# Attention logits split by heads over two steps, phi and the second weighing moved behind dense matmuls, in a kernel of linear-memory attention beside a token-mixing MLP

## The chip, the cores and the metric

The kernel runs on one core of one Trainium2 chip. The metric is the device time of one execution in microseconds (us). The core's engines are called as the profile calls them: PE is the matmul engine (PEld its weight loads), ACT the scalar engine, DVE the vector engine, POOL the one that makes the masks here, SP the one that issues most DMAs.

A ratio is the mean time of one kernel's runs over the mean of the other's of the same rounds, so it is not quite the ratio of the medians that are quoted beside it.

## The reference, cut to what matters

```python
def _A_ref(x, wq, wk, wv, wo, beta):           # x: 1 x 2048 x 1024, already normalised
    H, Dh, N, L = 32, 32, 4, 512               # 4 segments of 512 tokens
    q, k, v = ...                              # x @ wq, wk, wv, by heads and segments
    phi = lambda t: jnp.where(t > 0, t + 1.0, jnp.exp(t))
    M, z = 0, 0
    for s in range(N):
        logits = einsum('bhqd,bhkd->bhqk', qs, ks) * scale + mask     # causal inside the segment
        a_dot = softmax(logits) @ vs
        a_mem = (phi(qs) @ M) / (phi(qs) @ z + 1e-06)
        o = g * a_mem + (1.0 - g) * a_dot
        M = M + phi(ks)^T @ vs;  z = z + sum(phi(ks))
    return o @ wo
def _B_ref(x, w1, b1, w2, b2): ...             # LayerNorm, then gelu(w1) and w2 over the token axis
return x + _A_ref(xn, ...) + _B_ref(xn, ...)   # ... marks cuts
```

## The kernel before

After a head (LayerNorm and the first MLP product, up to 217 us) the kernel runs 32 *units*: one segment and a group of four heads each. A unit makes logits in two *steps*, exponentiates them on ACT, masks them on POOL, and weighs v in four *weighings* (one for each block of 128 queries), which DVE evicts. Two units ahead, q and k are projected, and v where needed. The gaps are filled with *dense* matmuls of 128x128 by 512 columns, from the second MLP product and from the product with wo (`main_emit(n)` emits n of them; `share(u)` says how many at each of three places). A tail ends the program.

Logits have a contraction of only 32, so four heads use four row groups of PE at once (`tile_position`). The kernel never lets two row groups write one PSUM bank at the same time (the prediction names the page that asks for this). Key block 2 (256 columns for each head) has two heads in a bank, hence the explicit wait:

```python
    LOGIT_STEPS = [[[(0, 2), (2, 2)], [(1, 0), (3, 0), (0, 0), (2, 0)], [(1, 2), (3, 2)]],
                   [[(0, 1), (1, 1), (2, 1), (3, 1), (0, 3), (1, 3), (2, 3), (3, 3)]]]

    def logits(self, u, step):

        fw = self.fw
        k = u % 3
        toks = []
        for group in self.LOGIT_STEPS[step]:
            if len(toks) == 2:
                fw.E["pe"].eng.wait_ge(toks[0].sem, toks[0].val)
            banks = self.R_bank[4:6] if group[0][1] == 2 else self.R_bank[0:4]
            with fw.group(reads=[self.R_kT[k], self.R_qT[k]], writes=banks) as grp:
                for r, kb in group:
                    n_q = SEG_L - P * kb
                    b, col = (4 + r // 2, 256 * (r % 2)) if kb == 2 else (r, 384 if kb == 3 else 0)
                    fw.mm(self.ps[:, b, col:col + n_q], self.kT[k][32 * r:32 * r + 32, kb * P:(kb + 1) * P],
                          self.qT[k][32 * r:32 * r + 32, kb * P:SEG_L],
                          start=True, stop=True, tile_position=(32 * r, 0))
            toks.append(grp.tok)
        heads = self.ps[:, 0:4, :]
        if step == 0:
            self.weights((0,), heads, self.R_bank[0:4])
            self.weights((2,), self.ps[:, 4:6, :].rearrange("p b (h q) -> p (b h) q", q=256), self.R_bank[4:6])
        else:
            self.weights((1, 3), heads, self.R_bank[0:4])

    def weights(self, kbs, src, R_src):
        fw = self.fw
        off, total = PT_OFF[kbs[0]], sum(SEG_L - P * kb for kb in kbs)
        fw.op("act", lambda e: e.activation(self.pT[:, :, off:off + total], src, ACT.Exp, scale=SCALE),
              reads=R_src, writes=[self.R_pTu[kb] for kb in kbs] + [self.R_pTd[kb] for kb in kbs])
        for kb in kbs:
            d = self.pT[:, :, PT_OFF[kb]:PT_OFF[kb] + P]
            fw.op("pool", lambda e: e.affine_select(d, d, pattern=[[0, 4], [1, P]], compare_op=ALU.is_ge,
                                                    fill=0.0, base=0, channel_multiplier=-1),
                  reads=[self.R_pTu[kb]], writes=[self.R_pTd[kb]])
```

Projections; phi follows directly (`phi` is two DVE operations on `etmp`):

```python
    def proj_q(self, u, b):
        fw = self.fw
        w, R_w = self.wq_ring.get(u)
        self.proj(w, R_w, u, b)
        k = u % 3
        fw.op("act", lambda e: e.activation(self.qT[k][:], self.bank(b), ACT.Copy),
              reads=[self.R_bank[b]], writes=[self.R_qT[k]])
        if u >= N_GRP:
            fw.op("act", lambda e: e.activation(self.etmp[0][:], self.bank(b), ACT.Exp),
                  reads=[self.R_bank[b]], writes=[self.R_etmp[0]])
            self.phi(self.pqT[k][:], self.R_pqT[k], self.qT[k][:], self.R_qT[k], 0)

    def proj_k(self, u, b):
        fw = self.fw
        w, R_w = self.wk_ring.get(u)
        self.proj(w, R_w, u, b)
        k = u % 3
        fw.op("dve", lambda e: e.tensor_copy(self.kT[k][:], self.bank(b)),
              reads=[self.R_bank[b]], writes=[self.R_kT[k]])
        if u // N_GRP < N_SEG - 1:
            fw.op("act", lambda e: e.activation(self.etmp[1][:], self.bank(b), ACT.Exp),
                  reads=[self.R_bank[b]], writes=[self.R_etmp[1]])
            self.phi(self.mtmp[1][:], self.R_mtmp[1], self.kT[k][:], self.R_kT[k], 1)
```

The loop over units and the shares (the parts around it are cut):

```python
        for u in range(N_UNIT):
            s = u // N_GRP
            un, m = u + self.LEAD, u // 4 + 1
            n0, n1, n2 = self.share(u)
            if u == N_GRP:
                wait = _after(*[self.R_xnT[c] for c in range(4)])
                self.oT[1] = self.xnT[0]
                self.R_oT[1] = [Res(f"oT1_{g}", wait) for g in range(N_GRP)]
            self.logits(u, 0)
            if u and last_of_seg(u - 1):
                self.o_transpose_dma(u - 1)
            self.main_emit(n0)
            if u and not last_of_seg(u - 1):
                self.combine(u - 1)
            self.logits(u, 1)
            if u + 1 < N_UNIT and (u + 1) // N_GRP < N_SEG - 1:
                self.k_transpose(u + 1)
            if u and not last_of_seg(u - 1):
                self.o_transpose_dma(u - 1)
            self.main_emit(n1)
            self.weigh(u, 0)
            self.weigh(u, 1)
            if un < N_UNIT:
                self.proj_q(un, 0)
            else:
                self.main_emit(8)
            self.weigh(u, 2)
            if m < 2 * N_SEG:
                self.proj_v(m, u % 4, 2)
            self.weigh(u, 3)
            if un < N_UNIT:
                self.proj_k(un, 1)
            if last_of_seg(u):
                self.combine(u)
            self.main_emit(n2)
    ...
    def share(u):
        if u < N_UNIT - 4:
            return (11, 14, 7) if u < N_GRP else (11, 15, 8)
        return (11, 16, 10) if u < N_UNIT - 2 else (11, 16, 4) if u < N_UNIT - 1 else (11, 13, 7)
```

The softmax here doesn't subtract the row's maximum and nothing guards it: scores larger than these inputs give would overflow.

## Time and profile before

| | before |
|---|---|
| time, three runs | 699.18, 700.11, 700.43 us (median 700.11) |
| span of the profiled run | 698.3 us |
| first real matmul | 7.20 us |
| first logits, unit 0 | 217.55 us |
| one middle unit (484.06 to 499.14) | 15.09 us |
| PE gap before the last transposes | 0.47 us |

From the page of the kernel before, part 1 (busy time and share by engine) and the shares of part 4 (the chain of waits that ended last):

```profile
PE 687.9 (99%) x4740; PEld 327.3 (47%) x4830; DVE 260.3 (37%) x581; ACT 273.9 (39%) x301; POOL 104.8 (15%) x156
...
PE 96%; DMA 1%; issue 1%; DVE 1%; SPq 1%
```

A busy PE isn't yet a full PE, because the ends of matmuls are modelled. Starts are measured. In the trace, dense matmuls that follow each other start 0.2158 us apart. "TensorE: Matmul & The Clock Gate" of the Trainium skill (Part 1) gives 215.7 ns for 512 columns at the warm clock, and this trace agrees. A middle unit has 58 of them (12.52 us), 40 weighing matmuls of 25 ns (1.01 us), eight small memory matmuls (0.45 us) and the logits (1.08 us), together 15.06 of the measured 15.09 us.

Two stretches of the timeline of PE before, with start, duration and count, show both logit steps of a unit:

```profile
483.74 0.38 PE L194 MATMUL ps_all<-gT,w2h_898 128*128 128x512 bf16 x1
484.06 0.63 PE L194 MATMUL ps_all<-qT_1551,kT_1554 32*128 32x256 bf16 x8
484.62 1.90 PE L194 MATMUL ps_all<-gT,w2h_898 128*128 128x512 bf16 x8
486.35 0.81 PE L194 MATMUL ps_all<-gT,w2h_897 128*128 128x512 bf16 x3
487.10 0.40 PE L194 MATMUL ps_all<-qT_1551,kT_1554 32*128 32x384 bf16 x8
487.43 0.82 PE L194 MATMUL ps_all<-gT,w2h_897 128*128 128x512 bf16 x3
```

Read each step from the end of the dense matmul ahead (its start plus 0.2158) to the start of the next dense one. Step 0: 483.74 + 0.22 = 483.96 to 484.62, 0.66 us. Step 1: 486.35 + 3 x 0.2158 = 487.00 to 487.43, 0.43 us. The first 0.10 us of each pass before the first logit matmul starts.

ACT before, groups by shape between 250 and 690 us (count, busy us, mean ns, then idle time before them):

```profile
L810 ACT ACTIVATE pT<-ps_all 128x2048 bf16<-128x2048 f32 x59 | 110.7, 1877 | 56.1 <-PE ps_all L194 55.1
L810 ACT ACTIVATE pT<-ps_all 128x1024 bf16<-128x1024 f32 x29 | 29.5, 1018 | 0.0
L746 ACT ACTIVATE etmp_1567<-ps_all 128x512 bf16<-128x512 f32 x24 | 14.2, 592 | 0.0
```

The tail before, PE and then DVE. PE is idle for 0.47 us because the transposes wait for `o_s`. On DVE a bias add (`stg`) and then the last evictions run ahead of the chain that makes it:

```profile
681.28 0.22 PE L194 MATMUL ps_all<-MZbf,pqT_1558 128*128 128x132 bf16 x1
681.33 2.97 PE L194 MATMUL ps_all<-wo_sb,xnT_70 128*128 128x512 bf16 x13
684.77 0.40 PE L200 MATMUL ps_all<-ident,o_s_1566 128*128 128x128 bf16 x4 [0.47 <-DVE o_s_1566 L890]
```

```profile
680.71 0.75 DVE L954 SCALAR_TENSOR_TENSOR stg_1573<-ps_all,b2c,stg_1573 128x512 bf16<-128x512 f32 x1 [1.00 <-PE ps_all L194]
681.38 0.76 DVE L848 CAST ost_1564<-ps_all 128x264 bf16<-128x264 f32 x2
...
684.28 0.43 DVE L890 TENSOR_TENSOR o_s_1566<-prod 128x512 bf16<-128x512 bf16 x1
```

The head before, weight loads of PE. Each load stands for one matmul, so loads 0.43 us apart mean half the clock. The ten warming matmuls (`warm`, zeros) are over at 5.5 us, and the first real ones, from 7.17, are slow as well, until about 9.9 us:

```profile
4.64 0.15 PEld L194 LDWEIGHTS ps_all<-warm 128*128 128x128 bf16 x1 [0.28 <-issue]
7.17 0.14 PEld L194 LDWEIGHTS ps_all<-h,w1early 128*128 128x128 bf16 x2 [2.37 <-DMA w1early<-in_B_w_dram]
7.58 0.15 PEld L194 LDWEIGHTS ps_all<-h,w1early 128*128 128x128 bf16 x1 [0.27 <-issue]
...
10.04 2.04 PEld L194 LDWEIGHTS ps_all<-h,w1early 128*128 128x128 bf16 x10 [0.19 <-issue]
```

### The profile page before, as it was taken

How to read it: one execution, taken by the hardware profiler on the slowest of the kernel's cores; microseconds unless marked ns; L12 is line 12 of the kernel's file. 1: busy time of each engine (PE TensorE's matmuls, PEld its weight loads, DVE VectorE, ACT ScalarE, POOL GpSimd, SP SyncE). 2: the span in 40 equal slices, each digit the busy share in tenths (PEclk: the TensorE clock that was granted, in tenths of full speed). 3: DMA queues.
4: the chain of work that ended last, by engine and by line, in shares of the span. 5: the costliest groups of instructions: out<-in, count | busy, mean ns of one | idle time of the engine just before them, and what ended most of it. 6: DMA issues, size and time to landing. Idle time of an engine off the chain costs nothing.

```text
span 698.3 us, 11182 instructions
## 1 busy us (share of the span) xinstructions
PE 687.9 (99%) x4740; PEld 327.3 (47%) x4830; DVE 260.3 (37%) x581; ACT 273.9 (39%) x301; POOL 104.8 (15%) x156
## 2 busy tenths in 40 slices
PE   8999999999999999999999999999999999999998
PEld 3444444444444444444444445444445444444444
DVE  6740000000012334333455545546545553444545
ACT  7531111112234445444455344455444345434440
POOL 2500000000001112211122211112211112211130
PEclk9999999999999999999999999999999999999999
DMA  8487774327036438457263634526273533445004
GB/s 307 116 194 182 167 211 119 93 60 140 1 119 134 102 72 137 102 101 139 46 137 79 129 87 93 128 52 131 63 150 79 97 95 73 113 77 121 19 21 136
DMA packets 210553, 77.17 MB, mean 111 GB/s; under 512 B 173128, under 2 KB 202824, under 8 KB 210504
## 3 DMA queue, kind: packets, MB, share of 16 engines
q1 hardware_dynamic: 210280, 76.29, 48.3%
q8 instruction: 38, 0.62, 0.4%
q10 hardware_dynamic: 224, 0.16, 0.1%
q14 instruction: 11, 0.09, 0.1%
HBM read 59.79 MB, written 5.24 MB: 93 GB/s over the span
## 4 chain that ended last, share of the span: by engine, by line
PE 96%; DMA 1%; issue 1%; DVE 1%; SPq 1%
PE ps_all L194 96%; DMA xin<-in_A_x_dram 1%; SPq L216 1%; DVE prod L886 0%; DVE stg_1573 L954 0%; DVE ost_1564 L848 0%; DVE h L661 0%; DVE o_s_1566 L890 0%; PE ps_all L200 0%; DVE srec L884 0%; DVE fin_7812 L1047 0%; DVE srec L883 0%; DVE srec L885 0%; DVE ln_mv L644 0%; DVE ln_st L622 0%
## 5 line engine op out<-in xcount | busy, mean ns | idle before, releaser
L810 ACT ACTIVATE pT<-ps_all 128x2048 bf16<-128x2048 f32 (+1 forms) x96 | 149.4, 1591 | 58.3 <-PE ps_all L194 57.2
L814 POOL TENSOR_SCALAR_AFFINE_SELECT pT<-pT 128x512 bf16<-128x512 bf16 x128 | 88.3, 703 | 554.8 <-ACT pT L810 553.7
L717 ACT ACTIVATE gT<-ps_all,b1c 128x512 bf16<-128x512 f32 x56 | 37.7, 689 | 139.3 <-PE ps_all L194 133.8
L755 DVE CAST kT_1554<-ps_all 128x512 bf16<-128x512 f32 x11 | 7.6, 690 | 170.6 <-PE ps_all L194 170.6
L194 PE MATMUL ps_all<-h,w1s_80 128*128 128x512 bf16 x251 | 55.6, 379 | 0.3
L194 PE MATMUL ps_all<-h,w1s_81 128*128 128x512 bf16 x251 | 55.6, 379 | 0.3
L194 PE MATMUL ps_all<-h,w1s_79 128*128 128x512 bf16 x250 | 55.4, 379 | 0.3
L194 PE MATMUL ps_all<-gT,w2h_897 128*128 128x512 bf16 x219 | 54.3, 380 | 0.4
L194 PE MATMUL ps_all<-gT,w2h_895 128*128 128x512 bf16 x221 | 53.7, 380 | 0.2
L194 PE MATMUL ps_all<-gT,w2h_896 128*128 128x512 bf16 x214 | 53.0, 380 | 0.6 <-issue 0.2
L194 PE MATMUL ps_all<-gT,w2h_898 128*128 128x512 bf16 x215 | 52.7, 379 | 0.5 <-issue 0.2
L848 DVE CAST ost_1563<-ps_all 128x264 bf16<-128x264 f32 (+1 forms) x64 | 23.8, 394 | 56.2 <-PE ps_all L194 56.0
L194 PEld LDWEIGHTS ps_all<-h,w1s_80 128*128 128x128 bf16 x256 | 25.0, 98 | 30.2
L194 PEld LDWEIGHTS ps_all<-h,w1s_79 128*128 128x128 bf16 x256 | 25.0, 98 | 30.2
L194 PEld LDWEIGHTS ps_all<-h,w1s_81 128*128 128x128 bf16 x256 | 25.0, 98 | 30.2
L848 DVE CAST ost_1564<-ps_all 128x264 bf16<-128x264 f32 (+1 forms) x64 | 23.7, 393 | 39.1 <-PE ps_all L194 38.9
L758 ACT ACTIVATE etmp_1568<-ps_all 128x512 bf16<-128x512 f32 x24 | 14.3, 597 | 58.8 <-DVE kT_1556 L755 20.7
L194 PEld LDWEIGHTS ps_all<-gT,w2h_898 128*128 128x128 bf16 x224 | 21.1, 98 | 25.5 <-issue 1.3
L194 PEld LDWEIGHTS ps_all<-gT,w2h_896 128*128 128x128 bf16 x224 | 20.9, 98 | 25.8 <-issue 1.7
L194 PEld LDWEIGHTS ps_all<-gT,w2h_895 128*128 128x128 bf16 x224 | 20.8, 98 | 25.2 <-issue 1.3
L194 PEld LDWEIGHTS ps_all<-gT,w2h_897 128*128 128x128 bf16 x224 | 20.7, 98 | 24.9 <-issue 1.3
L194 PE MATMUL ps_all<-wo_sb,oT_1571 128*128 128x512 bf16 x125 | 31.1, 379 | 0.2
(154 smaller groups left out, 843.7 us busy)
## 6 DMA issues: line engine op xcount, KB each, us to landing
w1s_81<-in_B_w_dram SPq DMA_DIRECT2D x4, 1024.0 KB, 5.8
w1s_79<-in_B_w_dram SPq DMA_DIRECT2D x4, 1024.0 KB, 5.6
w1s_80<-in_B_w_dram SPq DMA_DIRECT2D x4, 1024.0 KB, 5.7
wq_891<-in_A_wq_dram SPq DMA_DIRECT2D x16, 256.0 KB, 5.5
wq_892<-in_A_wq_dram SPq DMA_DIRECT2D x16, 256.0 KB, 3.5
wk_893<-in_A_wk_dram SPq DMA_DIRECT2D x16, 256.0 KB, 5.3
wk_894<-in_A_wk_dram SPq DMA_DIRECT2D x16, 256.0 KB, 3.8
w2h_895<-in_B_w_dram SPq DMA_DIRECT2D x8, 448.0 KB, 4.8
```

Source lines behind the costliest of these rows:

```text
L194: ins = self.nc.tensor.matmul(*args, **kwargs)
L216: ins = es.eng.dma_start(out_ap, in_ap, transpose=True) if transpose else es.eng.dma_start(out_ap, in_ap)
L717: fw.op("act", lambda e: e.activation(self.gT[:, fc, half * 512:(half + 1) * 512], self.bank(b), ACT.Gelu_apprx_tanh, bias=self.b1c[:, fc: ...
L755: fw.op("dve", lambda e: e.tensor_copy(self.kT[k][:], self.bank(b)), reads=[self.R_bank[b]], writes=[self.R_kT[k]])
L758: fw.op("act", lambda e: e.activation(self.etmp[1][:], self.bank(b), ACT.Exp), reads=[self.R_bank[b]], writes=[self.R_etmp[1]])
L810: fw.op("act", lambda e: e.activation(self.pT[:, :, off:off + total], src, ACT.Exp, scale=SCALE), reads=R_src, writes=[self.R_pTu[kb] for ...
L814: fw.op("pool", lambda e: e.affine_select(d, d, pattern=[[0, 4], [1, P]], compare_op=ALU.is_ge, fill=0.0, base=0, channel_multiplier=-1), ...
L848: fw.op("dve", lambda e: e.tensor_copy(dst, self.ps[:, b, 0:n * VW]), reads=[self.R_bank[b]], writes=[self.R_ost[o][qb]])
```

## The change

The intent is to take the semaphore wait out of the logits. Key block 2 is split by heads: heads 0 and 2 in step 0, heads 1 and 3 in step 1, so that within a step no bank has two row groups. Its exp is split with it, and step 1 now waits for both exps of step 0, so more dense matmuls stand between the steps. The exps for phi read q and k from SBUF, so their PSUM banks come free earlier. Phi itself and the second weighing move behind dense work. Besides, the shares now add up exactly to the 1088 dense matmuls that there are, and the first chunk of x comes by one DMA instead of two halves issued by SP and ACT. The diff, cut to its core (the bookkeeping of resources is left out):

```diff
@@
         for fp in range(N_FCH // 2):
             self.w1_ring.srcs.append(self.B_w1[:, fp * 256:(fp + 1) * 256].rearrange("(c p) f -> p c f", p=P))
         self.R_w1e = [Res(f"w1e{c}") for c in range(N_TCH)]
-        for h, issuer in enumerate(("sp", "act")):
-            fw.dma(self.xin[64 * h:64 * h + 64, 0, :], self.x_d[64 * h:64 * h + 64, 0, :],
-                   writes=[(self.R_xin[0], self.R_xin0)[h]], issuer=issuer)
         fw.op("act", lambda e: e.activation(self.junk[:, 0:1], self.warm[:, 0:1], ACT.Gelu_apprx_tanh),
               reads=[self.R_warm], writes=[self.R_junk])
-        for kind, c0, n in (("x", 1, 1), ("x", 2, 1), ("w", 0, 2), ("x", 3, 1), ("x", 4, 2), ("w", 2, 2), ("x", 6, 2),
+        for kind, c0, n in (("x", 0, 1), ("x", 1, 1), ("x", 2, 1), ("w", 0, 2), ("x", 3, 1), ("x", 4, 2), ("w", 2, 2), ("x", 6, 2),
                             ("w", 4, 4), ("x", 8, 4), ("w", 8, 4), ("x", 12, 4), ("w", 12, 4)):
             if kind == "x":
                 self.load_x(c0, n)
@@
         fw.op("act", lambda e: e.activation(self.qT[k][:], self.bank(b), ACT.Copy),
               reads=[self.R_bank[b]], writes=[self.R_qT[k]])
         if u >= N_GRP:
-            fw.op("act", lambda e: e.activation(self.etmp[0][:], self.bank(b), ACT.Exp),
-                  reads=[self.R_bank[b]], writes=[self.R_etmp[0]])
+            fw.op("act", lambda e: e.activation(self.etmp[0][:], self.qT[k][:], ACT.Exp),
+                  reads=[self.R_qT[k]], writes=[self.R_etmp[0]])
+
+    def phi_q(self, u):
+        if u >= N_GRP:
+            k = u % 3
             self.phi(self.pqT[k][:], self.R_pqT[k], self.qT[k][:], self.R_qT[k], 0)
 
     def proj_k(self, u, b):
@@
         fw.op("dve", lambda e: e.tensor_copy(self.kT[k][:], self.bank(b)),
               reads=[self.R_bank[b]], writes=[self.R_kT[k]])
         if u // N_GRP < N_SEG - 1:
-            fw.op("act", lambda e: e.activation(self.etmp[1][:], self.bank(b), ACT.Exp),
-                  reads=[self.R_bank[b]], writes=[self.R_etmp[1]])
+            fw.op("act", lambda e: e.activation(self.etmp[1][:], self.kT[k][:], ACT.Exp),
+                  reads=[self.R_kT[k]], writes=[self.R_etmp[1]])
+
+    def phi_k(self, u):
+        if u // N_GRP < N_SEG - 1:
+            k = u % 3
             self.phi(self.mtmp[1][:], self.R_mtmp[1], self.kT[k][:], self.R_kT[k], 1)
 
     def proj_v(self, m, c, b):
@@
 
 
 
-    LOGIT_STEPS = [[[(0, 2), (2, 2)], [(1, 0), (3, 0), (0, 0), (2, 0)], [(1, 2), (3, 2)]],
-                   [[(0, 1), (1, 1), (2, 1), (3, 1), (0, 3), (1, 3), (2, 3), (3, 3)]]]
+    LOGIT_STEPS = [[(0, 2), (2, 2), (1, 0), (3, 0), (0, 0), (2, 0)],
+                   [(1, 2), (3, 2), (0, 1), (2, 1), (1, 1), (3, 1), (0, 3), (2, 3), (1, 3), (3, 3)]]
 
     def logits(self, u, step):
 
         fw = self.fw
         k = u % 3
-        toks = []
-        for group in self.LOGIT_STEPS[step]:
-            if len(toks) == 2:
-                fw.E["pe"].eng.wait_ge(toks[0].sem, toks[0].val)
-            banks = self.R_bank[4:6] if group[0][1] == 2 else self.R_bank[0:4]
-            with fw.group(reads=[self.R_kT[k], self.R_qT[k]], writes=banks) as grp:
-                for r, kb in group:
-                    n_q = SEG_L - P * kb
-                    b, col = (4 + r // 2, 256 * (r % 2)) if kb == 2 else (r, 384 if kb == 3 else 0)
-                    fw.mm(self.ps[:, b, col:col + n_q], self.kT[k][32 * r:32 * r + 32, kb * P:(kb + 1) * P],
-                          self.qT[k][32 * r:32 * r + 32, kb * P:SEG_L],
-                          start=True, stop=True, tile_position=(32 * r, 0))
-            toks.append(grp.tok)
-        heads = self.ps[:, 0:4, :]
-        if step == 0:
-            self.weights((0,), heads, self.R_bank[0:4])
-            self.weights((2,), self.ps[:, 4:6, :].rearrange("p b (h q) -> p (b h) q", q=256), self.R_bank[4:6])
-        else:
-            self.weights((1, 3), heads, self.R_bank[0:4])
-
-    def weights(self, kbs, src, R_src):
-        fw = self.fw
-        off, total = PT_OFF[kbs[0]], sum(SEG_L - P * kb for kb in kbs)
-        fw.op("act", lambda e: e.activation(self.pT[:, :, off:off + total], src, ACT.Exp, scale=SCALE),
-              reads=R_src, writes=[self.R_pTu[kb] for kb in kbs] + [self.R_pTd[kb] for kb in kbs])
-        for kb in kbs:
+        with fw.group(reads=[self.R_kT[k], self.R_qT[k]], writes=self.R_bank[0:6]):
+            for r, kb in self.LOGIT_STEPS[step]:
+                n_q = SEG_L - P * kb
+                b, col = (4 + r // 2, 256 * (r % 2)) if kb == 2 else (r, 384 if kb == 3 else 0)
+                fw.mm(self.ps[:, b, col:col + n_q], self.kT[k][32 * r:32 * r + 32, kb * P:(kb + 1) * P],
+                      self.qT[k][32 * r:32 * r + 32, kb * P:SEG_L],
+                      start=True, stop=True, tile_position=(32 * r, 0))
+        self.weights(self.pT[:, step::2, 512:768], self.ps[:, 4:6, 256 * step:256 * step + 256], self.R_bank[4:6],
+                     [self.R_pTu[2], self.R_pTd[2]] if step == 0 else [self.R_pTu[4]])
+        kbs = ((0,), (1, 3))[step]
+        off = PT_OFF[kbs[0]]
+        self.weights(self.pT[:, :, off:off + 512], self.ps[:, 0:4, :], self.R_bank[0:4],
+                     [R[kb] for R in (self.R_pTu, self.R_pTd) for kb in kbs])
+        for kb in (kbs if step == 0 else (1, 2, 3)):
             d = self.pT[:, :, PT_OFF[kb]:PT_OFF[kb] + P]
             fw.op("pool", lambda e: e.affine_select(d, d, pattern=[[0, 4], [1, P]], compare_op=ALU.is_ge,
                                                     fill=0.0, base=0, channel_multiplier=-1),
-                  reads=[self.R_pTu[kb]], writes=[self.R_pTd[kb]])
+                  reads=[self.R_pTu[kb]] + ([self.R_pTu[4]] if kb == 2 else []), writes=[self.R_pTd[kb]])
+
+    def weights(self, dst, src, R_src, R_dst):
+        self.fw.op("act", lambda e: e.activation(dst, src, ACT.Exp, scale=SCALE), reads=R_src, writes=R_dst)
 
     def weigh(self, u, qb):
 
@@
         vA, R_vA = self.vA[i], self.R_vA[i]
         upd = qb == 3 and s < N_SEG - 1
         reads = [self.R_pTu[kb] for kb in range(qb + 1)] + [self.R_pTd[kb] for kb in range(qb + 1)]
+        if qb > 1:
+            reads += [self.R_pTu[4]]
         reads += R_vA if upd else R_vA[0:qb + 1]
         if s:
             reads += [self.R_pqT[k], self.R_MZbf[g]]
@@
             if u and last_of_seg(u - 1):
                 self.o_transpose_dma(u - 1)
             self.main_emit(n0)
+            if u + 1 < N_UNIT:
+                self.phi_k(u + 1)
             if u and not last_of_seg(u - 1):
                 self.combine(u - 1)
             self.logits(u, 1)
@@
                 self.o_transpose_dma(u - 1)
             self.main_emit(n1)
             self.weigh(u, 0)
-            self.weigh(u, 1)
             if un < N_UNIT:
                 self.proj_q(un, 0)
             else:
-                self.main_emit(8)
+                self.main_emit(6)
+            self.weigh(u, 1)
             self.weigh(u, 2)
             if m < 2 * N_SEG:
                 self.proj_v(m, u % 4, 2)
+            else:
+                self.main_emit(4)
             self.weigh(u, 3)
+            if un < N_UNIT:
+                self.phi_q(un)
             if un < N_UNIT:
                 self.proj_k(un, 1)
             if last_of_seg(u):
@@
     def share(u):
 
         if u < N_UNIT - 4:
-            return (11, 14, 7) if u < N_GRP else (11, 15, 8)
-        return (11, 16, 10) if u < N_UNIT - 2 else (11, 16, 4) if u < N_UNIT - 1 else (11, 13, 7)
+            return (14, 13, 5) if u < N_GRP else (14, 14, 6)
+        return (14, 12, 5) if u < N_UNIT - 2 else (13, 10, 3) if u < N_UNIT - 1 else (13, 10, 5)
 
     def tail(self):
         fw = self.fw
```

More of the change, by code (lines that the diff above doesn't have):

```diff
@@ L430, in alloc @@
         self.R_xin = [Res(f"xin{c}") for c in range(N_TCH)]
-        self.R_xin0 = Res("xin0b")
         self.R_junk, self.R_warm = Res("junk"), Res("warm")
@@ L492, in over_late @@
         self.R_pk = [R(f"pk{i}") for i in range(2)]
-        self.R_pTu = [R(f"pTu{k}") for k in range(4)]
+        self.R_pTu = [R(f"pTu{k}") for k in range(5)]
         self.R_pTd = [R(f"pTd{k}") for k in range(4)]
@@ L620, in stats_dve @@
         for h in halves:
-            reads = [self.R_xin[c]] + ([self.R_xin0] if c == 0 else [])
-            fw.op("dve", lambda e: e.bn_stats(st[:, 6 * h:6 * h + 6], src[:, 512 * h:512 * h + 512]), reads=reads,
-                  writes=[R])
+            fw.op("dve", lambda e: e.bn_stats(st[:, 6 * h:6 * h + 6], src[:, 512 * h:512 * h + 512]),
+                  reads=[self.R_xin[c]], writes=[R])
         if halves[-1]:
@@ L967, in attention_and_out @@
         self.proj_k(0, 5)
+        self.phi_k(0)
         self.k_transpose(0)
```

## The prediction

> **What bounds the kernel.** TensorE, almost without a gap. The page gives it 99% busy, but ends of matmuls are modelled, so I read start-to-start times in the timeline: 512-column matmuls start every 215.8 ns, 33-column weighings every 25 ns. A unit, first logits to next (484.06 to 499.14 us), takes 15.09 us. Its sum: 58 dense matmuls x 0.2158 = 12.52, weighing 1.01, memory read and update 0.45, logits 1.08: 15.06. Nothing waits there. The granted clock is 1.00, ACT 39% busy, DVE 37%. From 10 to 684 us I find one gap over 0.25 us, in the tail. "TensorE: Matmul & The Clock Gate" of the Trainium skill gives 215.7 ns warm; this trace agrees.
>
> **What the change does.**
> 1. *Logits.* Before, step 0 takes 0.657 us from the end of the dense matmul ahead to the start of the next, step 1 0.425. In step 0 heads 1 and 3 of key block 2 wait for a semaphore of heads 0 and 2, which share their banks ("TensorEngine Tiling", Gotcha 1, forbids two row tiles in one bank at once): they start at 0.443 where their rows were free at about 0.33. Moved to step 1, they lose that wait, but their 256 columns (0.108 us and a 0.011 us bubble) lengthen step 1's longest row. Estimate: 0.535 + 0.541 = 1.076 against 1.082 us: 0.2 us over 32 units.
> 2. *ACT.* One exp of 128x1024 (1.02 us) becomes two of 128x512 (0.59 each): +0.16 us a unit on an engine with spare time. Exp of q and k from SBUF stays near 0.6 us; it frees banks 0 and 1 earlier, for which no matmul waits now.
> 3. *Order.* Phi later, second weighing behind the projection of q, 14/13/5 dense matmuls instead of 11/14/7: same work, only slack moves. Step 1 must now wait for both exps of step 0: an estimated 2.55 us after dense work restarts, against 3.02 us of it. The bank of k is free 2.75 us after its projection began, against 3.0 (2.8 in units 6 and 7, the tightest). In the last two units the third weighing may wait 0.1 us for its mask. I allow 0.2 us of new stalls in all.
> 4. *Tail.* Before, the dense work ran out early (the shares exceed 1088), so none stood behind the last weighing: TensorE has a 0.63 us gap before the o transposes, waiting for DVE (a bias add of 0.75 us, eviction, combine). Now exactly 5 dense matmuls (1.08 us) stand there and the bias add follows the combine. The gap should vanish: -0.6 us.
> 5. *Head.* The first x chunk comes by one DMA instead of two halves, which landed at 3.43 (SP) and 3.95 us (ACT). One should land at about 3.75: -0.15 us, with the cold clock (430 ns matmuls until 9.8 us) as noise.
>
> **Sum.** -0.2 - 0.6 - 0.15 + 0.2 (stalls): about -0.8, from 700.1 (three runs scatter over 1.25). Predicted 699.2 us, range 697.9 to 700.6. Faster by over 2%: 1%; within 2%: 98%; slower by over 2%: 1%.
>
> **What would show it.** Logit steps near 0.53 and 0.54 us; unit distance 15.07 to 15.10; no gap before the last transposes; ACT busy +5 us; first real matmul at about 7.0 us.
>
> **What would make it wrong.** New waits for ACT or DVE at step 1, the second weighing or bank 1, once a unit (0.1 us each is 3 us); a transposed output too late for a segment's first product with wo; row groups that overlap less in the new order, at 0.1 us a unit; another phase of the clock gate at the start.

## The result, and the profile after

| | before | after |
|---|---|---|
| time, four runs of each | 698.85 to 700.43, median 699.64 us | 696.92 to 698.88, median 697.95 us |
| ratio (95% interval) | | 0.9975 (0.9954 to 0.9997) |
| span of the profiled run | 698.3 | 695.2 |

The change is faster by a quarter of a per cent. All outputs are right. The time lies at the lower edge of the predicted range (697.9). The gain was to be 0.9 us from the median of before (0.4 from the 699.64 of these rounds) and was about 1.7, so it was sized about half or less of what it is.

The page of the kernel after:

```profile
PE 685.3 (99%) x4746; PEld 326.5 (47%) x4830; DVE 257.2 (37%) x581; ACT 280.2 (40%) x333; POOL 100.1 (14%) x156
...
PE 98%; issue 1%; DMA 1%; DVE 0%; SPq 0%
```

The same part of a unit after, in PE's timeline:

```profile
481.41 0.38 PE L194 MATMUL ps_all<-gT,w2h 128*128 128x512 bf16 x1
481.72 0.50 PE L194 MATMUL ps_all<-qT,kT 32*128 32x256 bf16 x6
482.15 3.20 PE L194 MATMUL ps_all<-gT,w2h 128*128 128x512 bf16 x13
485.28 0.50 PE L194 MATMUL ps_all<-qT,kT 32*128 32x256 bf16 x10
485.71 0.60 PE L194 MATMUL ps_all<-gT,w2h 128*128 128x512 bf16 x2
```

Step 0 is now 481.63 to 482.15, 0.52 us. Step 1 begins after 14 dense matmuls (13 are recorded, one record is missing, as some are in every trace): 485.18 to 485.71, 0.53 us. Over all 32 units the medians from the trace's starts are 0.525 and 0.528 us, against 0.657 and 0.4255: 0.029 us less a unit.

ACT after, first the timeline and then the groups. The two exps of step 0 end at 484.63, 2.48 us after dense work restarted, and step 1 comes at 485.28, so they are hidden. The exps for phi read SBUF now:

```profile
482.26 2.37 ACT L810 ACTIVATE pT<-ps_all 128x512 bf16<-128x512 f32 x2 [0.30 <-PE ps_all L194]
```

```profile
L810 ACT ACTIVATE pT<-ps_all 128x2048 bf16<-128x2048 f32 x59 | 110.4, 1872 | 0.0
L810 ACT ACTIVATE pT<-ps_all 128x512 bf16<-128x512 f32 x58 | 34.6, 597 | 72.0 <-PE ps_all L194 72.0
L741 ACT ACTIVATE etmp<-qT 128x512 bf16<-128x512 bf16 x24 | 15.1, 629 | 0.8
```

The tail after, PE and DVE. Five more dense matmuls stand behind the last weighing (19 by their starts, 14 before, one of each without a record), the transposes don't wait, and the bias add comes after `o_s`:

```profile
677.47 0.22 PE L194 MATMUL ps_all<-MZbf,pqT 128*128 128x132 bf16 x1
677.74 1.02 PE L194 MATMUL ps_all<-wo_sb,oT 128*128 128x512 bf16 x4
678.60 3.18 PE L194 MATMUL ps_all<-wo_sb,xnT 128*128 128x512 bf16 x14
681.62 0.39 PE L200 MATMUL ps_all<-ident,o_s 128*128 128x128 bf16 x4
```

```profile
677.72 0.43 DVE L844 CAST ost<-ps_all 128x264 bf16<-128x264 f32 x1 [0.90 <-PE ps_all L194]
...
680.30 0.43 DVE L886 TENSOR_TENSOR o_s<-prod 128x512 bf16<-128x512 bf16 x1
680.64 0.75 DVE L950 SCALAR_TENSOR_TENSOR stg<-ps_all,b2c,stg 128x512 bf16<-128x512 f32 x1
```

The head after. Sixteen loads take 3.15 us from the first real one on, 0.2 us each: no real matmul ran at half the clock in this execution.

```profile
4.64 0.15 PEld L194 LDWEIGHTS ps_all<-warm 128*128 128x128 bf16 x1 [0.28 <-issue]
6.80 3.15 PEld L194 LDWEIGHTS ps_all<-h,w1early 128*128 128x128 bf16 x16 [2.00 <-DMA w1early<-in_B_w_dram]
```

Where the 3.17 us between the two profiled spans lie, from start times in both traces:

| stretch | before | after | difference |
|---|---|---|---|
| to the first real matmul | 7.20 | 6.83 | -0.37 |
| first part of the first MLP product (while x still arrives) | 28.96 | 27.62 | -1.34 (clock) |
| rest of the first MLP product, to the first logits | 181.40 | 181.40 | 0.00 |
| units 0 to 27 | 416.51 | 415.60 | -0.90 |
| unit 28 to the first transpose | 50.71 | 50.17 | -0.54 |
| from there to the end | 13.55 | 13.54 | -0.02 |

So the profiled pair flatters the change by 1.34 us. That part is a matter of the clock at the start, and the fastest run of the changed kernel happened to be profiled. What is left, 1.83 us, had to be tested: which of the edits earn it, and what the reorder is for.

### The profile page after: what moved, and what is told of

The parts are those of the page before. It is cut to its first block, busy times and chain, and to the rows that moved or that the text cites. A ratio compares the mean times of both kernels' runs of the same rounds, so it can differ in the third digit from the quotient of the medians.

```text
span 695.2 us, 11228 instructions
## 1 busy us (share of the span) xinstructions
PE 685.3 (99%) x4746; PEld 326.5 (47%) x4830; DVE 257.2 (37%) x581; ACT 280.2 (40%) x333; POOL 100.1 (14%) x156
## 4 chain that ended last, share of the span: by engine, by line
PE 98%; issue 1%; DMA 1%; DVE 0%; SPq 0%
PE ps_all L194 98%; DMA xin<-in_A_x_dram 1%; SPq L216 0%; DVE ln_st L617 0%; DVE h L656 0%; DVE fin L1050 0%; PE ps_all L200 0%
## 5 line engine op out<-in xcount | busy, mean ns | idle before, releaser
L194 PE MATMUL ps_all<-gT,w2h 128*128 128x512 bf16 x868 | 207.8, 380 | 1.6 <-issue 0.2
L810 ACT ACTIVATE pT<-ps_all 128x512 bf16<-128x512 f32 (+1 forms) x128 | 151.4, 1235 | 76.7 <-PE ps_all L194 76.7
L194 PE MATMUL ps_all<-h,w1s 128*128 128x512 bf16 x752 | 165.1, 379 | 0.8
L194 PEld LDWEIGHTS ps_all<-gT,w2h 128*128 128x128 bf16 x896 | 83.2, 98 | 105.6 <-issue 13.8
L194 PEld LDWEIGHTS ps_all<-h,w1s 128*128 128x128 bf16 x768 | 75.1, 98 | 90.6
L844 DVE CAST ost<-ps_all 128x264 bf16<-128x264 f32 (+1 forms) x128 | 49.2, 398 | 169.4 <-PE ps_all L194 169.4
L194 PE MATMUL ps_all<-xnT,wk 128*128 128x512 bf16 x256 | 60.5, 379 | 0.0
L194 PE MATMUL ps_all<-xnT,wq 128*128 128x512 bf16 x256 | 60.4, 378 | 0.0
L194 PE MATMUL ps_all<-wv_sb,xnT 128*128 128x512 bf16 x227 | 54.0, 379 | 1.6
L194 PE MATMUL ps_all<-vA,pT 128*128 128x33 bf16 x1280 | 48.6, 177 | 0.0
```

The costliest lines, as they stand in the source:

```text
L194: ins = self.nc.tensor.matmul(*args, **kwargs)
L810: self.fw.op("act", lambda e: e.activation(dst, src, ACT.Exp, scale=SCALE), reads=R_src, writes=R_dst)
L844: fw.op("dve", lambda e: e.tensor_copy(dst, self.ps[:, b, 0:n * VW]), reads=[self.R_bank[b]], writes=[self.R_ost[o][qb]])
```

## The experiments

Two things make small differences readable. One is the *stretch*, from the first logits of unit 0 to the end of the span, worked out from each trace. It leaves the head and its clock out, and it repeats to 0.04 us (480.77, 480.73 and 480.73 us in the three traces of kernels that share this part with the one before, 479.31 to 479.32 in four that share it with the changed one). The other is a head in which the clock does not vary, which the first group of runs found. Names ending in `_w` have that head. Each group of runs was on one chip beside runs of the kernel before, but the groups were on different chips, so times of different groups agree only to some tenths of a us; the ratios are within a group.

### 1. The head: one DMA, and the clock

Theory A: the single DMA lets PE start 0.4 us earlier, and apart from that the number of slow real matmuls is chance. Rival B: the earlier data is what made the clock go up in time.

`head_only` is the kernel before with this edit:

```diff
-        for h, issuer in enumerate(("sp", "act")):
-            fw.dma(self.xin[64 * h:64 * h + 64, 0, :], ..., issuer=issuer)
-        for kind, c0, n in (("x", 1, 1), ("x", 2, 1), ...
+        for kind, c0, n in (("x", 0, 1), ("x", 1, 1), ("x", 2, 1), ...
```

> The kernel before with the first x chunk loaded by one DMA. Theory A (head = an early landing plus luck with the clock): the first real matmul starts at 6.8 us instead of 7.2 (-0.37), whatever the clock does; the number of real matmuls that still run at 430 ns varies from run to run (0 or about 6, 1.3 us), in this kernel as in the one before, so its five times fall into two groups about 1.3 us apart, and the mean gains 0.4 us. Rival B (the single DMA causes the warm clock): no cold matmul in the profile and all times in the lower group, mean gain 1.0 us or more.

Measured: 698.54, 698.47, 700.84, 700.08, 698.49, 700.50, mean 699.49, against a mean of 699.60 for before in the same rounds; ratio 0.9999 (0.9983 to 1.0015). Two groups, as A has it, so B falls. But the mean gained 0.1 us and not 0.4; with an interval of more than 1 us to each side, it can't tell the two apart. PE did start at 6.61 us, yet then it stood idle once more, by the view for the next of the first MLP weights (its first logits came at 216.08 us, 0.20 before those of before_warm13, a run of the same group):

```profile
6.58 3.15 PEld L194 LDWEIGHTS ps_all<-h,w1early 128*128 128x128 bf16 x16 [1.79 <-DMA w1early<-in_B_w_dram]
10.49 1.42 PEld L194 LDWEIGHTS ps_all<-h,w1early 128*128 128x128 bf16 x8 [0.76 <-DMA w1early<-in_B_w_dram]
```

Within the lower group it is 0.2 to 0.3 us faster than the lower group of before (698.71 to 698.75, with two more at 699.15 and 699.29).

`after_two_halves` puts the two half DMAs back into the changed kernel (the same edit, reversed).

> The changed kernel with the two half DMAs back. A: first real matmul at 7.2 us again, mean 0.4 us above the changed kernel; times in two groups 1.3 us apart. B: always about 6 cold matmuls, 1.7 us above the changed kernel.

Measured: 698.97, 697.36, 698.86, 699.42, 697.60, 697.58, mean 698.30; ratio to before 0.9982 (0.9968 to 0.9996). Two groups again. The profiled run, of the upper group, started at 7.35 us and had six real matmuls 0.427 us apart. Its lower group (697.4 to 697.6) is about 0.5 us above that of the changed kernel in other rounds (696.9 to 697.3).

`before_warm13` and `after_warm13` change one constant, so that the warming matmuls last until 6.8 us if all of them run slow. Theory A' is about when the clock goes up:

```diff
-    N_WARM = 10
+    N_WARM = 13
```

> The kernel before with 13 instead of 10 warming matmuls, which fill TensorE up to about 6.8 us. Theory A': [...]filling the 1.7 us hole before the real matmuls makes it go up before they start or soon after, so at most 2 or 3 cold real matmuls in any run, times in one group near the lower group of before (about 699.0), mean gain 0.5 to 0.8 us. Rival: the clock's phase has nothing to do with the hole; still two groups 1.3 us apart and no gain of the mean.

> The changed kernel with 13 warming matmuls. A': one group near 697.0, 2.4 to 2.8 us below the mean of before; but if all 13 run cold they end at 6.80 us, just at the first real matmul (6.83), so no loss from that. Rival: two groups, 697.0 and 698.7, as the changed kernel itself has.

Measured: before_warm13 698.52 to 699.01 (median 698.77, ratio to before 0.9990, 0.9975 to 1.0004). after_warm13 696.94 to 697.60 (median 697.11, ratio to before 0.9966, 0.9953 to 0.9979). Each is one group. In the trace of after_warm13 the step up falls among the warming matmuls:

```profile
4.21 0.15 PEld L194 LDWEIGHTS ps_all<-warm 128*128 128x128 bf16 x1 [0.28 <-issue]
4.64 0.78 PEld L194 LDWEIGHTS ps_all<-warm 128*128 128x128 bf16 x4 [0.28 <-issue]
6.81 3.15 PEld L194 LDWEIGHTS ps_all<-h,w1early 128*128 128x128 bf16 x16 [1.40 <-DMA w1early<-in_B_w_dram]
```

In all nine profiles with 13 warming matmuls no real matmul ran slow, though the step came at different times: in six of them among the warming matmuls, from 4.2 us on, and in three not before the thirteenth, which started at 6.35 us. In the five profiles with 10, two had six or seven slow ones, and those two runs are of the upper groups. "TensorE: Matmul & The Clock Gate" (Part 1: The HAM clock gate) explains it by a free-running window of about 3.4 us that must be busy. The runs fit this in part: the step does come at varying times, but in before_warm13 it came at about 4.2 us (by starts at 3.79, 4.20 and 4.41 us), 2.9 us after the first matmul of the trace. A window of 3.4 us that must be busy from end to end doesn't fit this run.

Nor is it the hole before the real matmuls that has to be filled, as the expectations say. With 13, PE still had nothing to do for 0.2 to 1.8 us there, as in before_warm13, whose 22 real matmuls shown are about 0.22 us apart all the same:

```profile
1.25 4.40 PE L194 MATMUL ps_all<-warm 128*128 128x512 bf16 x13 [1.25 <-DVE brow L518]
7.21 4.96 PE L194 MATMUL ps_all<-h,w1early 128*128 128x512 bf16 x22 [1.56 <-DMA w1early<-in_B_w_dram]
```

In after_phi_early_w (1.8 us by starts) and before_warm13 (1.7 us), and in the changed kernel itself with 10 (1.7 us), the clock had gone up before the hole, and the real matmuls were fast. In the kernel before with 10, with the same 1.7 us, it had not, and they were slow. What 13 bring is more time for the step to come before the real work does. The runs show the two outcomes and the cure, not the window itself. The slow matmuls account for 1.3 to 1.5 us in the traces; the means of the two groups lie 1.5 to 2.0 us apart in these kernels, and what makes the rest stays open.

With the clock out of the way the change is worth 1.6 us (means of 698.80 and 697.20 us, 0.23%), or 1.75 by the spans of the two profiles (697.01 and 695.26).

### 2. The parts of the change, one at a time

All have the 13 warming matmuls. The yardsticks are before_warm13 (stretch 480.73 us, 698.8 us) and after_warm13 (479.32 us, 697.1 us).

`after_old_logits_w` is the changed kernel with `LOGIT_STEPS`, `logits` and `weights` of before. Theory A says that the logits earn 0.93 us, the rival that the order does.

> The changed kernel with 13 warming matmuls and the old logits (semaphore wait in step 0, one exp of 128x1024); order, shares, exps from SBUF and single DMA kept. A: steps 0.656 and 0.425 again, unit distance 15.09, no new wait: 0.93 us above the changed kernel with 13 warming matmuls (697.1), so 698.0. B': if the order itself brought the 0.9 us, 697.1.

Measured: 698.00 to 698.66 us, stretch 480.18 us, so 0.86 us above the changed kernel, with steps of 0.655 and 0.426 us and units of 15.09 us. The logits earn 0.86 of the 1.41 us of the stretch. (The time rose by 1.1 us in the means, against runs on another chip; the rest is in the head, which in this trace was 0.8 us later.)

`before_tail_w` is the kernel before with shares that add up to 1088:

```diff
-        return (11, 16, 10) if u < N_UNIT - 2 else ...
+        return (11, 16, 6) if u < N_UNIT - 2 else ...
```

> The kernel before with 13 warming matmuls, and 6 instead of 10 dense matmuls at the end of units 28 and 29, so that the shares add up to exactly 1088 and 7 dense matmuls stand behind the last weighing. Theory A: the gap before the o transposes goes (0.41 us by the wait that the profile of before shows; the 0.63 us that I predicted held one unrecorded matmul of 0.22): 698.4 against 698.8 without it, and the bias add lies behind the combine on DVE. B: no change, the wait comes back elsewhere in the tail: 698.8.

Measured: 698.40 to 698.79 us, stretch 480.29 us: 0.44 us less than before_warm13, and no wait before the transposes is left in its waits. So the tail earns 0.44 of the stretch. The time went down only by 0.2 us in the means, because the head of this run was later (first logits at 216.74 and not 216.28 us). That is why the stretch is the measure here.

0.86 and 0.44 leave 0.11 us. It is one wait: the first product with wo in unit 8 came 0.116 us late in the trace of before, and unit 8 took 15.206 us where its neighbours take 15.09 to 15.10. After, it is 15.059. The place of phi is the likely cause, since the combine of unit 7 no longer stands behind phi of k on DVE. In before_warm13 the combine starts 0.95 us after the first logits of unit 8 and its output lands at 4.44, in after_warm13 at -0.37 and 3.14, for a product that is due at 4.43. In the run below that puts phi of q and k back, a wait of 0.56 us (by starts) for the transfer of that output appears at the same product. But no run moves phi of k alone, and the margin is thin: in logits_only_w, with phi in its old place and the earlier units slower, the output lands at 4.32, and this wait is gone, too.

`logits_only_w` is the other side: the kernel before with the new logits only, in the old order and with the old shares.

> The kernel before with 13 warming matmuls and the new logits, but the old order and shares (11 dense matmuls between the steps). Theory A (the logits gain 29 ns a unit, and need the reorder to keep it): step 0 is 0.525 us, but step 1 now waits for both exps of step 0, which end 2.48 us after dense work restarts (changed kernel's trace), against 11 x 0.2158 = 2.37: about 0.15 to 0.2 us of wait in each unit, 5 to 6 us in all, minus 0.9: near 703.5 against 698.8 for the same without the new logits. Rival B (the split of the logits is the gain by itself): 697.9, unit distance 15.06.

Measured: 702.23 to 702.74 us, ratio to before 1.0040 (1.0023 to 1.0057), stretch 484.03 us: 3.3 us slower than before_warm13, although step 0 takes 0.525 us as in the changed kernel (0.65 in the first units). The direction of A is right, the size too large. Step 1 waits, but only 0.05 us a unit. In the weight loads of PE it is the difference between 0.42 us, the usual idle time before logits, and this:

```profile
352.56 0.22 PEld L194 LDWEIGHTS ps_all<-qT,kT 32*128 32x128 bf16 x10 [0.47 <-ACT pT L807]
```

Most of the loss is in the first eight units, 0.33 us each, and in the last one, 0.36, which the expectation didn't have. From unit 9 on the others lose about 0.02 each. In the first eight, step 0 starts 0.12 us later, and the second weighing waits 0.19 us, both by start-to-start times. The mask for it comes later now, because a second exp runs ahead.

`after_n0_11_w` moves only the dense matmuls back: 11 between the steps, and the difference behind step 1 (the line for the last four units, cut here, changes likewise).

```diff
-            return (14, 13, 5) if u < N_GRP else (14, 14, 6)
+            return (11, 16, 5) if u < N_GRP else (11, 17, 6)
...
```

> The changed kernel with 13 warming matmuls and 11 instead of 14 dense matmuls between the two logit steps (3 more behind step 1). Theory A (the shift to 14 hides the second exp of step 0): 0.05 us of wait for ACT in each unit, as in the run with the new logits alone: 1.5 us slower than 697.1. B (0.15 to 0.2 us a unit, as I first reckoned from the end of the exps): 5 us slower. C (no effect): 697.1.

Measured: 698.97 to 699.10 us, stretch 480.83 us, 1.51 us above the changed kernel: 0.05 us a unit, as A has it. So three dense matmuls more between the steps are worth more than what the logits themselves gained.

### 3. Is the rest of the reorder needed?

The prediction had said of the order that only slack moves. In the changed kernel, that is so. Whether it is needed can be seen by undoing one part at a time.

`after_exp_psum_w` reads q and k from PSUM again in the two exps (the edit for k is shown):

```diff
-            ... activation(self.etmp[1][:], self.kT[k][:], ACT.Exp), reads=[self.R_kT[k]], ...
+            ... activation(self.etmp[1][:], self.bank(b), ACT.Exp), reads=[self.R_bank[b]], ...
```

> The changed kernel with 13 warming matmuls, exp of q and k from PSUM again. A (needed by the new order): bank 1 is then free only after the exp of k, about 3.35 us after the projection of k began, where the next logits want it after 3.02 (2.81 in the first units): about 0.3 to 0.4 us of wait in 22 units, 7 to 9 us: near 705. B (as my prediction had it: no matmul waits for these banks): 697.1.

Measured: 707.21 to 708.03 us, ratio 1.0111 (1.0094 to 1.0129), stretch 489.55 us, 10.2 us more. A unit with an exp of k loses 0.41 us (15.475 and 15.063), one of the first eight 0.55. Units 22 to 31 lose nothing, because no k after unit 23 needs phi. From its timeline:

```profile
350.33 0.68 DVE L754 CAST kT<-ps_all 128x512 bf16<-128x512 f32 x1
...
351.11 0.60 ACT L757 ACTIVATE etmp<-ps_all 128x512 bf16<-128x512 f32 x1 [2.68 <-PE ps_all L194]
...
351.85 0.50 PE L194 MATMUL ps_all<-qT,kT 32*128 32x256 bf16 x6 [0.34 <-ACT etmp L757]
```

The logits want bank 1, and it is read by the exp until 351.71. Read from SBUF, the bank would have been free at 351.01, when DVE had copied it. The exp itself is slower from SBUF (629 against 592 ns for q). "Perfetto Trace Analysis" of the Trainium skill (Optimizing Scalar/DVE Operations) has about 93 ns of overhead for SBUF against 51 for PSUM, a difference of 42; here it is 37. That is no test of the page: it adds that profiled latencies are about twice its figures, and here the source is also bf16 in SBUF and f32 in PSUM. The 37 ns are paid on an engine with time to spare.

`after_weigh_early_w` puts the second weighing directly behind the first again.

```diff
             self.weigh(u, 0)
+            self.weigh(u, 1)
             if un < N_UNIT:
                 self.proj_q(un, 0)
             else:
                 self.main_emit(6)
-            self.weigh(u, 1)
             self.weigh(u, 2)
```

> The changed kernel with 13 warming matmuls, second weighing directly behind the first again. A: it then wants the mask of key block 1, which lands about 3.15 us after dense work restarts, where the weighing is due after about 2.96 (13 matmuls, units 0 to 7) or 3.2 (14): 0.2 us of wait in 8 units, up to 0.1 in the rest: 1 to 3 us slower than 697.1. B (order moves nothing): 697.1.

Measured: 707.74 to 708.30 us, ratio 1.0119 (1.0102 to 1.0136), stretch 489.88 us, 10.6 us more, where 1 to 3 were expected. It is the wait that A named, but larger: 0.13 us in a middle unit, 0.40 in each of the first eight, 0.6 to 1.0 in units 28 to 31, and three single units with 0.4 to 0.8. In the first units the masks start at 237.77 us and PE could weigh again at 238.55:

```profile
237.77 1.81 POOL L805 TENSOR_SCALAR_AFFINE_SELECT pT<-pT 128x512 bf16<-128x512 bf16 x3 [2.93 <-ACT pT L810]
...
238.04 0.26 PE L194 MATMUL ps_all<-vA,pT 128*128 128x33 bf16 x4
...
238.55 0.36 PE L194 MATMUL ps_all<-vA,pT 128*128 128x33 bf16 x8 [0.26 <-POOL pT L805]
```

Of these, the list of waits shows only those that its modelled ends leave visible ("PE waits for POOL, 6.0 us in 15 waits"). The stretch has the whole.

`after_phi_early_w` puts phi directly behind the projections again (`phi_q(un)` after `proj_q(un, 0)`, `phi_k(un)` after `proj_k(un, 1)`).

> The changed kernel with 13 warming matmuls, phi of q directly behind the projection of q and phi of k behind that of k again. Theory A (the new place of the second weighing makes the old place of phi harmful): DVE, in program order, now waits for the exp of q before it may evict the second weighing, and the fourth weighing needs that bank: 0.4 to 0.6 us of wait in 24 units, 10 to 14 us: near 709. B (as predicted: only slack moves): 697.1.

Measured: 714.64 to 715.63 us, ratio 1.0212 (1.0199 to 1.0225), stretch 497.11 us, 17.8 us more. Units that compute phi of q, from unit 6 on, lose 0.6 to 0.66 us each, unit 8 1.2, units 28 and 29 1.5. In order on DVE:

```profile
343.55 0.63 ACT L741 ACTIVATE etmp<-qT 128x512 bf16<-128x512 bf16 x1
344.21 0.29 DVE L721 TENSOR_SCALAR mtmp<-etmp 128x512 bf16<-128x512 bf16 x1 [2.58 <-ACT etmp L741]
344.54 0.69 DVE L723 SCALAR_TENSOR_TENSOR pqT<-qT,mtmp 128x512 bf16<-128x512 bf16 x1
345.15 0.77 DVE L844 CAST ost<-ps_all 128x264 bf16<-128x264 f32 x2
...
345.72 0.46 PE L194 MATMUL ps_all<-vA,pT 128*128 128x33 bf16 x12 [0.49 <-DVE ost L844]
```

DVE sits idle for 2.58 us, waiting for the exp of q. The second and third weighing end near 343.0 and 343.4 us, but their evictions stand behind phi and start at 345.15, and the fourth weighing waits for the bank. So this is not a busy DVE but an order on DVE: moving the second weighing behind the projection of q makes it necessary to move phi, too.

### 4. The changed kernel again

> The changed kernel unchanged, on this chip. Theory A: two groups of times, near 697.1 and 698.6, by whether real matmuls ran before the clock went up; its mean minus that of the same with 13 warming matmuls (697.1) is 0.5 to 1.0 us. B: all near 697.1.

Measured: 697.05, 696.95, 696.92, 698.91, 698.69, 696.89, mean 697.57; ratio to before in these rounds 0.9963 (0.9949 to 0.9977). Two groups, as A has it. The ratio looks better than the first 0.9975 because before fell into its upper group in 9 of its 11 runs here. Over all rounds together before was in the lower group (under 699.5) in 13 of 33 runs, the changed kernel in 6 of 10 (under 698); these numbers don't tell whether the odds differ between the kernels.

The best version is after_warm13, the change with 13 warming matmuls: mean 697.20 us, 1.6 us below the kernel before with the same head and 2.4 below before itself (699.60, same rounds). Ten runs of the changed kernel, of other rounds, have a mean of 697.71 and a spread of 2 us instead of 0.7.

One idea was not run. An order of the logits with 640 columns in every row of both steps might be shorter still, going by the columns alone, but it needs two row groups in one bank without a semaphore between them, which both kernels avoid.

## Why the prediction was right or wrong

- **What bounds the kernel: right.** PE without gaps, unit by unit. All runs agree: what adds no wait and takes no time from PE moves nothing.
- **Logits: right in mechanism, wrong in size.** This is the step that failed most: "Estimate: 0.535 + 0.541 = 1.076 against 1.082 us: 0.2 us over 32 units". Measured 0.525 + 0.528 = 1.053, and 0.86 us when undone. Of the two terms, step 0 was 0.010 too long because I took the time back to dense work from the old step 0 (0.102 us after the last column), where it is 0.090 here. Step 1 was 0.013 too long, because I charged a bubble of 0.011 behind both pieces of the row and the same return. Together 0.023 us a unit, which 32 units make 0.7 us. For the 256 columns and their bubble 0.119 us were charged to step 1, and it grew by 0.103; step 0 was to lose 0.122 us and lost 0.132.
- **ACT: right.** Busy 6.3 us more (5 predicted), no matmul waits for it.
- **Order: right that nothing waits in the changed kernel, wrong in the allowance.** "I allow 0.2 us of new stalls in all": there were none, and an old one of 0.11 us in unit 8 went, below the 0.25 us that I had listed as gaps. The phrase "only slack moves" was also too weak a reading. The slack moved to just where the new logits need it: without one of the three moves the kernel is 10 to 18 us slower, without the shift of three dense matmuls 1.5 us. One such place is the bank of k: 0.41 us a unit when the exp stays on PSUM.
- **Tail: right, a little too large.** 0.6 predicted, 0.44 measured. That "none stood behind the last weighing" holds only for the shares: 14 matmuls of the tail's own product stood there, too few to hide DVE's chain. With five more, and the bias add behind the chain, it is hidden. The gap of 0.63 us that I took from starts held one dense matmul without a record (0.22 us); the profile's own wait had 0.47.
- **Head: right in sign in the pairs compared, its size open, and incomplete.** The first real matmul came 0.37 us earlier (0.15 predicted), 0.33 us of which is left at the first logits in the pair with 13 warming matmuls. One pair doesn't settle this: over all traces without slow matmuls the first logits come at 215.85 to 216.78 us with the single DMA (nine traces) and at 216.28 to 216.74 with the two halves (three), and the means of the same pair, 1.60 us apart, leave only 0.2 for the head beside the 1.41 of the stretch. In the mean of head_only only 0.1 us shows. What the prediction left out is that the single DMA also lets SP issue the first MLP weights sooner (at 2.19 instead of 2.51 us), and PE needs them, too. The clock was put down as noise without a size. It is a choice between two outcomes 1.5 to 2 us apart, larger than everything predicted together.
- **The sum:** predicted -0.2 - 0.6 - 0.15 + 0.2 = -0.8. Measured with the clock held, from the traces: -0.86 (logits) - 0.44 (tail) - 0.11 (unit 8) - 0.33 (head) = -1.74, against a difference of the spans of 1.75. The sum has to come out, since the 0.11 and the 0.33 were read as what is left in this pair of traces; the 0.86 and the 0.44 were measured by runs of their own.

## What to carry to other kernels

Where one engine has no gaps, sum what it does in one iteration from start times, and treat ten nanoseconds of an iteration as a term of the sum: rounding up both halves of a difference of 29 ns hid three quarters of this gain. An edit that shortens the bounding engine's work and lengthens a chain on another engine has to come with the order that hides the chain, so judge the parts by undoing them one by one in the whole, not by adding one to the old kernel. For effects under half a per cent, first make the start of the kernel repeatable (here by enough warming matmuls that the clock is up before the data are there), and compare stretches of the traces beside the times.

## What the Trainium skill lacked or had wrong

- "TensorE: Matmul & The Clock Gate" has the busy window and its chance position, but no case of a warm-up of over 4 us that comes too late. Here ten warming matmuls (4.3 us when slow) gave two groups of times 1.5 to 2 us apart, and 13 one group with a spread of 0.5 to 0.7 us. Its window of about 3.4 us of sustained work is too strict for before_warm13, where the clock went up 2.9 us after the first matmul.
- "TensorEngine Tiling (Array Packing)" says under Key Properties that a change of tiling mode drains the engine, without a cost. Here 0.095 us pass from the end of a dense matmul to the first of the 32-row matmuls, and 0.09 to 0.10 us on the way back: about 0.19 us for each visit, two visits a unit. How much of that is the drain, no run shows.
- The same page (Gotcha 1) says that two row tiles may not be in one bank at once and leaves the ordering to software, without its price: with a semaphore, the second pair here started 0.236 us after the first pair's last column, 0.12 us after its rows were free.
- "Perfetto Trace Analysis" is not contradicted where it was used, nor confirmed: 37 ns more for an exp of 128x512 from SBUF (bf16) than from PSUM (f32), where its two overheads differ by 42.
